# Weights kept as (high, low) pairs: the load of a weight tile takes every second element of 1024 bytes

## The chip, the cores and the metric

The kernel runs on one core of one Trainium2 chip. The metric is the device time of one execution in microseconds. The kernel before took 657.98 us (median of 3 runs, 657.59 to 659.76).

## The reference

Three layers follow each other; the matrices are float32 in the reference's arithmetic.

```python
# linear attention, q k v: (8, 8, 576, 64)
kv  = einsum('bhsd,bhse->bhde', softmax(k, over s), v)
x   = einsum('bhsd,bhde->bhse', softmax(q, over d), kv)   # -> 4608 tokens x 512
# feed-forward with a cosine gate, w_in: 512 x 2048, w_out: 2048 x 512
h = x @ w_in
x = (h * cos(h)) @ w_out
# soft mixture: 8 experts x 4 slots, w1: 512 x 1024, w2: 1024 x 512 each
logits = x @ phi
slot_input = softmax(logits, over tokens).T @ x
out = softmax(logits, over slots) @ experts(slot_input)
```

Only the product `h = x @ w_in` (4608 x 512 by 512 x 2048) touches the change.

## The kernel before, in words

The tokens are cut into nine blocks of 512. Stage by stage: block `b` of the attention gives a tile of x with 512 columns (tokens) and four chunks of 128 rows (`kk`); then sixteen steps follow, one for each 128 columns of `w_in` (`f`, 0 to 15). A step computes one 128 x 512 tile of `h` in PSUM (`mm1`, L925), rounds it, takes the fractional part, its cosine, and the product (L933 to L949); the results are the tile `G`, which feeds the logits (L963) and the weighted sums over tokens (L1110). The ninth block is worked in two halves of 256 tokens each, with tiles called `xe` instead of `XH` and `XL`. That is 8 x 16 steps with 512 columns and 2 x 16 with 256.

The product of a step is done in a three-term form. Both x and w are split into a high part (rounded to the type fp32r) and a low part (what the rounding left). For each chunk `kk` three matmuls add into the same PSUM tile: high w with high x, high w with low x, low w with high x. So a step is 4 x 3 = 12 matmuls, and each of them has a load of 128 x 128 weights of its own. In all there are 160 x 12 = 1920 loads and matmuls on L925: 1536 with 512 columns and 384 with 256.

The weights lie in eight tiles `W0` to `W7`, each of 256 columns of `w_in`, [128 partitions, 2 parts, 4 chunks, 256 columns]. A load of weights (`lhsT` on L925) reads 128 neighbouring elements of 4 bytes in each partition, that is 512 bytes.

How the W tiles come about: the weights arrive as 64-bit floats (two 32-bit words for each number). `conv_wi` turns 128 columns of them (one `f`) into 32-bit floats in a piece of the tile `A`; that takes a pass on ScalarE (L780), one on ScalarE or GpSimd that works on the neighbouring words of the raw data (L791, L795), and one on VectorE (L805). Then part 3 (L818, ScalarE) rounds `A` into the high part of W, and part 4 (L820, VectorE or GpSimd) subtracts that from `A` and writes the low part. There are sixteen of each, one for each `f`, between 19.7 and about 90 us; in this time the first block's steps run too.

What sets the order: every operation has a place in a list (`PLACES`), and the program is issued in the order of these places; which engine an operation takes is listed beside it (the string for `cD`, part 4, is "DDPPPDPDDPPPPPPP": D for VectorE, P for GpSimd). Waits between engines follow from the bytes that the operations read and write. For instance `cD` of f=7 has place 273, and the step of f=6 has 285; both touch the tile `W3`. A change of layout changes no place and no engine.

Of the kernel before, what the change touches and what calls it, by code (L numbers as in the profile page):

```python
# [10 lines left out]
F32 = mybir.dt.float32  # L11
F32R = mybir.dt.float32r
# [267 lines left out]
def attention_cosine_moe_softmoe(  # L280
# [21 lines left out]
    nc = tc.nc  # L302
# [10 lines left out]
    def sbt(shape, tag, dt=F32, bufs=1, name=None):  # L313
        if tag in PADS and tag not in PADDED:
            PADDED.add(tag)
            sb.tile([128, PADS[tag] // 4], F32, tag=f"pad{tag}", name=f"pad{tag}", bufs=1)
        return sb.tile(shape, dt, tag=tag, name=name or tag, bufs=bufs)

    def pst(tag, bufs):
        return ps.tile([128, 512], F32, tag=tag, name="ps_" + tag, bufs=bufs)  # L320
# [44 lines left out]
    w_t, xe = {}, []  # L365
# [402 lines left out]
    def convert(src, y, i, how):  # L768

        z = y.bitcast(I32)
        if not wide:
            if i == 0:
                nc.vector.tensor_copy(y, src[..., 0])
        elif i == 0:
            nc.scalar.activation(  # L780
                out=y, in_=src[..., 1].bitcast(F32), func=ACTF.Prelu, scale=2.0 ** -112,
                alpha=-(2.0 ** 32),
            )
        elif i == 1 and how == "DVE":
            nc.vector.tensor_scalar(
                out=z, in0=z, scalar1=3, scalar2=None, op0=ALU.logical_shift_left
            )
        elif i == 1:
            upper = src.bitcast(U16)[..., 1]
            if how == "ACT":  # L790
                nc.scalar.activation(  # L791
                    out=src[..., 0], in_=upper, func=ACTF.Identity, scale=2.0 ** -13, bias=low
                )
            else:
                nc.gpsimd.tensor_scalar(  # L795
                    out=src[..., 0], in0=upper, scalar1=2.0 ** -13, scalar2=LOW, op0=ALU.mult,
                    op1=ALU.add,
                )
        elif how == "DVE":
            nc.vector.scalar_tensor_tensor(  # L800
                out=z, in0=src[..., 0], scalar=29, in1=z, op0=ALU.logical_shift_right,
                op1=ALU.bitwise_or,
            )
        else:
            nc.vector.scalar_tensor_tensor(  # L805
                out=z, in0=z, scalar=3, in1=src[..., 0], op0=ALU.logical_shift_left,
                op1=ALU.bitwise_or,
            )

    def conv_wi(f, part, how):  # L810
        j, o = divmod(f, 2)
        o = slice(128 * o, 128 * o + 128)
        src = raw["i", j].rearrange("p k (f t) -> p k f t", t=RW)[:, :, o]
        t = abuf[:, 2 + f % 2].rearrange("p (k f) -> p k f", k=4)
        if part == 3:
            if j not in w_t:
                w_t[j] = sbt([128, 2, 4, 256], f"W{j}", F32R)
            nc.scalar.copy(out=w_t[j][:, 0, :, o], in_=t)  # L818
        elif part == 4:
            (nc.gpsimd if how == "POOL" else nc.vector).tensor_tensor(  # L820
                out=w_t[j][:, 1, :, o], in0=t, in1=w_t[j][:, 0, :, o].bitcast(F32),
                op=ALU.subtract,
            )
        else:
            convert(src, t, part, how)
# [63 lines left out]
    u_t, t_t, lt_t = {}, {}, {}  # L889
# [4 lines left out]
    def tile_of(d, i):  # L894

        return (i + (12 if 0 < d < 8 and d % 2 == 0 else 8 if d == 8 else 0)) % NF
# [14 lines left out]
    def mm1(s, ks):  # L911
        d, f = divmod(s, NF)
        b, t0, nt = parts[d]
        f = tile_of(d, f)
        if ks[0] == 0:
            u_t[s] = pst("h", 3)[:, 0:nt]
        w = w_t[f // 2]
        o = 128 * (f % 2)
        x = (
            (xh[b % 2], xl[b % 2]) if nt == 512  # L920
            else [xe[t0 // 256][:, i] for i in range(2)]
        )
        for kk in ks:
            for n, (wi, xi) in enumerate(((0, 0), (0, 1), (1, 0))):
                nc.tensor.matmul(  # L925
                    out=u_t[s], lhsT=w[:, wi, kk, o:o + 128], rhs=x[xi][:, kk],
                    start=(kk == 0 and n == 0), stop=(kk == 3 and n == 2),
                )

# [648 lines left out]
    def conv_ops():  # L1578
# [4 lines left out]
        for j, (ti, to) in enumerate(tags):  # L1583
            for kind, tag, load in (("i", ti, load_wi), ("o", to, load_wo)):
                mine = [(("cB" if kind == "i" else "oB"), f) for f in (2 * j, 2 * j + 1)]
                op(("lw" + kind, j), DMA, 2.75 if kind == "i" else 2.58, load, j, tag, more=LATE,
                   after=hold(tag, *mine))
            for f in (2 * j, 2 * j + 1):
                narrow("c", f, conv_wi, [("lwi", j), past("cD", f - 2)])
                op(("cH", f), ACT, 0.52, conv_wi, f, 3, ACT,  # L1590
                   after=[("cB", f)] + (hold(f"W{j}") if f % 2 == 0 else [("cH", f - 1)]))
                op(("cD", f), None, 0, conv_wi, f, 4, after=[("cH", f)],
                   ways=[(POOL, 1.26, True, ()), (DVE, 0.61, True, ())])
                narrow("o", f, conv_wo, [("lwo", j), past("w2_tr", f - 4), past("oW", f - 4)])
                op(("oW", f), DMA, 0.66, conv_wo, f, 3, None, more=LATE,
                   after=[("oB", f)])
                op(("w2_tr", f), PE, 0.47, w2_tr, f, take="m", after=[("oB", f)])
                op(("w2_tr_ev", f), None, 0, w2_tr_ev, f, give="m",
                   ways=[(ACT, 0.48, False, ()), (DVE, 0.6, False, ())],
                   after=[("w2_tr", f), past("w2_mm", j - 1)])  # L1600
            op(("w2_mm", j), PE, 0.52, w2_mm, j, take="m",
               after=[("w2_tr_ev", 2 * j), ("w2_tr_ev", 2 * j + 1), ("phi",), past("w2_ev", j - 1)])
            op(("w2_mm_ev", j), None, 0, w2_mm_ev, j,
               ways=[(ACT, 0.27, False, ()), (DVE, 0.33, False, ())],
               after=[("w2_mm", j), past("w2_sum", j - 2)])
            op(("w2_sum", j), PE, 0.35, w2_sum, j, duty=0.3, after=[("w2_mm_ev", j)])
            op(("w2_ev", j), DVE, 0.13, w2_ev, j, give="m", after=[("w2_sum", j)])
# [4 lines left out]
    def step_ops(s):  # L1612
# [13 lines left out]
        for ks in ((0,), (1,), (2,), (3,)) if s == 0 else (range(4),):  # L1626
            op(("mm1", s) if ks[-1] == 3 else ("mm1", s, ks[-1]), PE,
               (0.7 if nt == 512 else 0.355) * len(ks),
               mm1, s, ks, take=None if ks[0] else "h",
               after=[("x_lo", b, kk) for kk in ks] * (f == 0) + [past("cD", w)] * (b == 0)  # L1630
               + [("mm1", s, ks[0] - 1) if ks[0] else past("mm1", s - 1)]
               + [past("g", s - 3)] * (ks[0] == 0))
# [246 lines left out]
```

## Time and profile before

| | before |
|---|---|
| time, median of 3 runs | 657.98 us |
| the profiled execution's own time | 659.31 us |
| its span, first to last instruction | 657.4 us |
| mean granted TensorE clock in it | 0.986 |
| TensorE matmul (PE) busy | 625.2 us, 95% |
| TensorE weight loads (PEld) busy | 472.3 us, 72% |
| VectorE (DVE) busy | 534.9 us, 81% |
| ScalarE (ACT) busy | 365.6 us, 56% |
| GpSimd (POOL) busy | 128.2 us, 20% |

Busy times of PE and PEld overlap: a load of weights is recorded while the matmul before it runs. An instruction's recorded duration holds its latency, so that neighbours overlap; the pace of a stream is read from the starts of its instructions. The profiled execution's own time is 1.9 us above its span, and 1.33 us above the median of the runs.

### The profile page before, as it was taken

What the parts mean: (1) busy time and instruction counts of PE and PEld (TensorE: products, weight loads), DVE (VectorE), ACT (ScalarE), POOL (GpSimd) and SP (SyncE); (2) the same over time, 40 slices, a digit from 0 to 9 for tenths busy, and PEclk for the clock granted to TensorE, in tenths of its full rate; (3) what the DMA queues carried; (4) which work ended last, traced back from release to release, by engine and by line L of the source; (5) the groups of instructions that cost most, each with busy time, mean ns of one, the idle gap of its engine ahead of it and who ended that gap; (6) DMA issues with size and microseconds to landing.
All of it is one profiled execution on the core that took longest, in us unless ns stands there. A gap on an engine that the chain in (4) does not pass through costs nothing.

```text
span 657.4 us, 18204 instructions
## 1 busy us (share of the span) xinstructions
PE 625.2 (95%) x7745; PEld 472.3 (72%) x7745; DVE 534.9 (81%) x1075; ACT 365.6 (56%) x642; POOL 128.2 (20%) x131
## 2 busy tenths in 40 slices
PE   5999999999999999999999999999999999999990
PEld 4677777687868777877788788778878889853540
DVE  7889999989998988979979887878988888852251
ACT  4899988576465376446456452443645465530051
POOL 4435546052132043040230101001110000000000
PEclk9799999999999999999999999999999999999996
DMA  9998955264312242143212400013001518899968
GB/s 320 304 408 291 351 163 148 98 154 128 91 49 76 80 114 82 49 113 99 67 31 67 138 0 2 1 37 94 1 1 48 211 35 332 328 386 412 421 242 347
DMA packets 60992, 103.88 MB, mean 158 GB/s; under 512 B 9456, under 2 KB 40560, under 8 KB 55920
## 3 DMA queue, kind: packets, MB, share of 16 engines
q1 hardware_dynamic: 60912, 102.74, 45.9%
q8 instruction: 60, 0.98, 0.6%
q14 instruction: 20, 0.16, 0.1%
HBM read 88.15 MB, written 14.57 MB: 156 GB/s over the span
## 4 chain that ended last, share of the span: by engine, by line
PE 80%; DMA 7%; DVE 6%; ACT 2%; issue 1%; POOL 1%; SPq 0%; DVEq 0%; ACTq 0%
PE ps_h L925 54%; PE ps_m L1110 6%; PE ps_LT L963 4%; PE ps_m L713 2%; PE ps_m L528 2%; PE ps_m L1357 2%; DMA rwo<-in_moe_w_out_dram 2%; DMA Q<-in_q_dram 2%; PE ps_LT L1699 2%; DMA KVB<-in_k_dram 1%; DMA out_dram<-ob 1%; DMA G<-in_moe_w_out_dram 1%; PE ps_h L1315 1%; PE ps_m L1315 1%; DVE qm L422 1%
## 5 line engine op out<-in xcount | busy, mean ns | idle before, releaser
L925 PE MATMUL ps_h<-XH,W 128*128 128x512 f32 x1024 | 330.1, 397 | 2.2 <-DVE G L949 2.2
L925 PEld LDWEIGHTS ps_h<-XH,W 128*128 128x128 f32 x1024 | 192.3, 188 | 56.8 <-issue 7.1
L925 PE MATMUL ps_h<-XL,W 128*128 128x512 f32 x512 | 201.0, 393 | 0.0
L946 ACT ACTIVATE T<-T 128x512 f32<-128x512 f32 (+1 forms) x160 | 92.7, 587 | 90.8 <-DVE T L941 90.4
L933 ACT ACTIVATE T<-ps_h,quarter 128x512 int32<-128x512 f32 (+1 forms) x123 | 79.3, 646 | 87.0 <-PE ps_h L925 86.6
L949 DVE TENSOR_TENSOR G<-T,ps_h 128x512 f32<-128x512 f32 (+1 forms) x160 | 99.2, 623 | 21.0 <-ACT T L946 15.7
L925 PEld LDWEIGHTS ps_h<-XL,W 128*128 128x128 f32 x512 | 96.2, 188 | 20.0
L941 DVE SCALAR_TENSOR_TENSOR T<-T,ps_h 128x512 f32<-128x512 int32 (+1 forms) x160 | 98.9, 622 | 10.6 <-ACT T L933 9.4
L970 DVE STREAM_TRANSPOSE G<-G 128x512 f32<-128x512 f32 (+1 forms) x160 | 98.2, 637 | 0.3 <-PE ps_LT L963 0.2
L425 POOL TENSOR_TENSOR Q<-Q,qm 128x512 f32<-128x512 f32 x33 | 34.8, 1072 | 153.7 <-DVE qm L422 128.2
L689 POOL TENSOR_TENSOR KVB<-KVB,km 128x576 f32<-128x576 f32 x22 | 33.3, 1539 | 72.3 <-DVE km L682 51.3
L925 PE MATMUL ps_h<-xe,W 128*128 128x256 f32 x384 | 46.7, 281 | 0.0
L925 PEld LDWEIGHTS ps_h<-xe,W 128*128 128x128 f32 x384 | 45.3, 189 | 1.6 <-DVE G L949 0.8
L446 POOL TENSOR_TENSOR Q<-Q,qm 128x512 f32<-128x512 f32 x27 | 27.9, 1061 | 82.6 <-DVE qm L439 63.3
L963 PE MATMUL ps_LT<-G,wphi 128*32 128x128 f32 (+1 forms) x1280 | 38.7, 264 | 0.8 <-issue 0.8
L963 PEld LDWEIGHTS ps_LT<-G,wphi 128*32 128x32 f32 x1280 | 30.4, 109 | 8.9 <-issue 6.7
L1110 PE MATMUL ps_m<-G,A 32*32 32x512 f32 x1024 | 35.7, 597 | 0.0
L946 ACT ACT_TABLE_LOAD x24 | 30.8, 1283 | 0.4
L935 DVE TENSOR_SCALAR T<-ps_h 128x512 int32<-128x512 f32 (+1 forms) x37 | 22.7, 614 | 7.1 <-PE ps_h L925 6.9
L422 DVE TENSOR_REDUCE qm<-Q 128x8 f32<-128x512 f32 x36 | 24.0, 672 | 3.2 <-DMA Q<-in_q_dram 3.2
L1110 PEld LDWEIGHTS ps_m<-G,A 32*32 32x32 f32 x1024 | 16.9, 103 | 13.4 <-issue 8.1
L1128 DVE SCALAR_TENSOR_TENSOR gacc<-gacc,ac,ps_m 128x512 f32<-128x512 f32 x32 | 23.2, 732 | 2.3 <-PE ps_m L1110 2.3
(214 smaller groups left out, 715.6 us busy)
## 6 DMA issues: line engine op xcount, KB each, us to landing
w_u<-in_moe_w_dram SPq DMA_DIRECT2D x22, 1024.0 KB, 8.1
KVB<-in_k_dram SPq DMA_DIRECT2D x16, 576.0 KB, 5.1
KVB<-in_v_dram SPq DMA_DIRECT2D x32, 256.0 KB, 4.4
out_dram<-ob SPq DMA_DIRECT2D x8, 1024.0 KB, 8.9
rwi<-in_moe_w_in_dram SPq DMA_DIRECT2D x7, 1024.0 KB, 9.9
G<-in_moe_w_dram SPq DMA_DIRECT2D x7, 1024.0 KB, 7.0
rwo<-in_moe_w_out_dram SPq DMA_DIRECT2D x5, 1024.0 KB, 10.5
wo<-G SPq DMA_DIRECT2D x16, 256.0 KB, 4.5
```

The lines of the kernel that those rows point to most:

```text
L422: nc.vector.reduce_max(out=qm[:, t], in_=qv(t), axis=AX.X)
L425: (nc.vector if eng == "DVE" else nc.gpsimd).tensor_tensor(out=qv(t), in0=qv(t), in1=qm[:, t].unsqueeze(2).to_broadcast([128, 8, 64]), op= ...
L446: (nc.vector if eng == "DVE" else nc.gpsimd).tensor_tensor(out=qv(t), in0=qv(t), in1=qs[:, t].unsqueeze(2).to_broadcast([128, 8, 64]), op= ...
L689: (nc.vector if eng == "DVE" else nc.gpsimd).tensor_tensor(out=k_t[:, t], in0=k_t[:, t], in1=km[:, t].unsqueeze(1).to_broadcast([128, KC, ...
L925: nc.tensor.matmul(out=u_t[s], lhsT=w[:, wi, kk, o:o + 128], rhs=x[xi][:, kk], start=(kk == 0 and n == 0), stop=(kk == 3 and n == 2),)
L933: nc.scalar.activation(out=t.bitcast(I32), in_=u_t[s], func=ACTF.Identity, bias=quarter)
L941: nc.vector.scalar_tensor_tensor(out=t, in0=t.bitcast(I32), scalar=0.25, in1=u_t[s], op0=ALU.subtract, op1=ALU.subtract)
L946: nc.scalar.activation(out=t_t[s], in_=t_t[s], func=ACTF.Sin, scale=-UNDER_TWO_PI)
L949: nc.vector.tensor_tensor(out=g_of(s), in0=t_t.pop(s), in1=u_t.pop(s), op=ALU.mult)
L963: nc.tensor.matmul(out=lt_t[d][32 * c:32 * c + 32, 0:w], lhsT=w2sb[:, f], rhs=g[:, w * c:w * c + w], start=(f0 == 0), stop=(f0 == NF - 1),)
L970: nc.vector.transpose(out=g_of(s), in_=g_of(s))
L1110: nc.tensor.matmul(out=st["gp"][i][32 * c:32 * c + 32].rearrange("p (f b) -> p f b", f=NF) if d < NB else st["gp"][i][32 * c:32 * c + 32]. ...
```

## The change

The two parts become the innermost dimension of the W tiles: for each weight its high and its low part lie side by side, 4 bytes each. The size of a tile, its place, the number of instructions, their order and their engines stay. A load of weights now reads 128 elements with a step of two elements (8 bytes) over 1024 bytes; part 3 writes with that step, and part 4 reads one of its two inputs and writes with it.

```diff
         if part == 3:
             if j not in w_t:
-                w_t[j] = sbt([128, 2, 4, 256], f"W{j}", F32R)
-            nc.scalar.copy(out=w_t[j][:, 0, :, o], in_=t)
+                w_t[j] = sbt([128, 4, 256, 2], f"W{j}", F32R)
+            nc.scalar.copy(out=w_t[j][:, :, o, 0], in_=t)
         elif part == 4:
             (nc.gpsimd if how == "POOL" else nc.vector).tensor_tensor(
-                out=w_t[j][:, 1, :, o], in0=t, in1=w_t[j][:, 0, :, o].bitcast(F32),
+                out=w_t[j][:, :, o, 1], in0=t, in1=w_t[j].bitcast(F32)[:, :, o, 0],
                 op=ALU.subtract,
             )
...
         for kk in ks:
             for n, (wi, xi) in enumerate(((0, 0), (0, 1), (1, 0))):
                 nc.tensor.matmul(
-                    out=u_t[s], lhsT=w[:, wi, kk, o:o + 128], rhs=x[xi][:, kk],
+                    out=u_t[s], lhsT=w[:, kk, o:o + 128, wi], rhs=x[xi][:, kk],
                     start=(kk == 0 and n == 0), stop=(kk == 3 and n == 2),
                 )
```

## Rows read from the trace of the kernel before

**Rows 1.** The page: busy time of each engine; chain that ended last, by line.

```profile
PE 625.2 (95%) x7745; PEld 472.3 (72%) x7745; DVE 534.9 (81%) x1075; ACT 365.6 (56%) x642; POOL 128.2 (20%) x131
...
PE ps_h L925 54%; PE ps_m L1110 6%; PE ps_LT L963 4%; PE ps_m L713 2%; PE ps_m L528 2%; PE ps_m L1357 2%; DMA rwo<-in_moe_w_out_dram 2%; DMA Q<-in_q_dram 2%; PE ps_LT L1699 2%; DMA KVB<-in_k_dram 1%; DMA out_dram<-ob 1%; DMA G<-in_moe_w_out_dram 1%; PE ps_h L1315 1%; PE ps_m L1315 1%; DVE qm L422 1%
```

**Rows 2.** Stages: stretch, its us, busy us of engines, clock, DMA share, GB/s.

```profile
31.20:60.00 28.80, 28.02 (x158) 21.03 (x155) 26.65 (x48) 27.23 (x50) 12.41 (x14) 1.00 0.96 359
60.00:90.00 30.00, 30.00 (x383) 22.98 (x382) 29.38 (x56) 29.94 (x54) 15.57 (x13) 1.00 0.92 305
...
516.50:576.00 59.50, 59.50 (x848) 53.63 (x850) 50.74 (x140) 33.06 (x77) 0.00 (x0) 1.00 0.63 232
```

**Rows 3.** Weight loads by columns: busy us, mean ns of one, idle before.

```profile
L925 PEld LDWEIGHTS ps_h<-XH,W 128*128 128x128 f32 x1024 | 192.3, 188 | 56.8 <-issue 7.1 <-DVE G L949 5.0 <-DVE A L618 0.8
...
L925 PEld LDWEIGHTS ps_h<-xe,W 128*128 128x128 f32 x384 | 45.3, 189 | 1.6 <-DVE G L949 0.8 <-DVE cm L1152 0.2 <-issue 0.2
L963 PEld LDWEIGHTS ps_LT<-G,wphi 128*32 128x32 f32 x1280 | 30.4, 109 | 8.9 <-issue 6.7 <-DMA wo<-G 0.4
```

**Rows 4.** PE's timeline, first block's step f=8: start, us, what, count.

```profile
64.64 0.63 PE L925 MATMUL ps_h<-XH,W 128*128 128x512 f32 x2
65.10 0.39 PE L925 MATMUL ps_h<-XL,W 128*128 128x512 f32 x1
65.34 0.63 PE L925 MATMUL ps_h<-XH,W 128*128 128x512 f32 x2
```

**Rows 5.** PE's timeline, second block.

```profile
150.12 0.62 PE L925 MATMUL ps_h<-XH,W 128*128 128x512 f32 x2
150.57 0.39 PE L925 MATMUL ps_h<-XL,W 128*128 128x512 f32 x1
150.80 0.62 PE L925 MATMUL ps_h<-XH,W 128*128 128x512 f32 x2
```

**Rows 6.** PE's timeline, ninth block, 256 columns.

```profile
539.66 12.99 PE L925 MATMUL ps_h<-xe,W 128*128 128x256 f32 x108
552.58 1.10 PE L963 MATMUL ps_LT<-G,wphi 128*32 128x64 f32 x64
```

**Rows 7.** PE's timeline, transposes: two narrow windows of eight in a row.

```profile
40.74 0.49 PE L849 MATMUL ps_m<-ident,G 128*128 128x128 f32 x3
...
40.96 0.49 PE L849 MATMUL ps_m<-ident,G 128*128 128x128 f32 x3
```

**Rows 8.** The conversion's instructions by line: busy us, mean ns, idle before.

```profile
L820 POOL TENSOR_TENSOR W<-A,W 128x512 fp32r<-128x512 f32 x11 | 14.6, 1331 | 21.1 <-ACT W L818 17.5 <-DMA Q<-in_q_dram 3.4
L805 DVE SCALAR_TENSOR_TENSOR A<-A,rwi 128x512 int32<-128x512 int32 x14 | 10.1, 728 | 0.0
...
L818 ACT CAST W<-A 128x512 fp32r<-128x512 f32 x16 | 9.8, 617 | 1.6 <-DVE A L805 1.5
...
L791 ACT ACTIVATE rwi<-rwi,low 128x512 int32<-128x512 uint16 x8 | 6.1, 762 | 0.0
...
L820 DVE TENSOR_TENSOR W<-A,W 128x512 fp32r<-128x512 f32 x5 | 3.4, 683 | 0.2 <-ACT W L818 0.2
```

**Rows 9.** GpSimd's timeline, 22 to 46 us, of L453 and L820.

```profile
22.14 2.15 POOL L453 TENSOR_TENSOR B<-Q,qm 128x512 f32<-128x512 f32 x1 [7.25 <-PE ps_m L466]
...
44.20 1.30 POOL L820 TENSOR_TENSOR W<-A,W 128x512 fp32r<-128x512 f32 x1
```

**Rows 10.** PE's timeline, steps f=3 and f=4, around the start of f=4.

```profile
45.13 0.63 PE L925 MATMUL ps_h<-XH,W 128*128 128x512 f32 x2
45.60 0.39 PE L925 MATMUL ps_h<-XL,W 128*128 128x512 f32 x1
45.83 0.63 PE L925 MATMUL ps_h<-XH,W 128*128 128x512 f32 x2
```

**Rows 11.** PE's timeline, step f=6 from 55.58, and VectorE's, the low part of f=7.

```profile
55.58 0.50 PE L925 MATMUL ps_h<-XH,W 128*128 128x512 f32 x1
55.91 0.40 PE L925 MATMUL ps_h<-XL,W 128*128 128x512 f32 x1
56.15 0.63 PE L925 MATMUL ps_h<-XH,W 128*128 128x512 f32 x2
...
56.57 0.68 DVE L820 TENSOR_TENSOR W<-A,W 128x512 fp32r<-128x512 f32 x1
```

## The prediction

> **What bounds the kernel now.** Read the page's busy line first: TensorE's matmuls are busy for 95% of the span, and the chain that ended last runs for 54% of the span over L925, the very matmuls whose weights are re-laid [rows 1]. The reader should see that the change sits in the loop that sets the time. Then the stages: in the ninth block (516.5 to 576.0) PE is busy 59.50 of 59.50 us while VectorE, the next, has 50.74; whatever a pair of load and matmul loses there goes to the end in full. From 60 to 90 us PE and ScalarE are both full (30.00 and 29.94 of 30.00), and this is where half of the conversion runs [rows 2]. Last, the pace of the pairs, read from starts of matmuls, since their durations overlap. With 512 columns three pairs take 65.34 - 64.64 = 0.70 us in one block, 233 ns a pair [rows 4], and 150.80 - 150.12 = 0.68 us in another, 227 ns [rows 5]. With 256 columns 108 pairs take 552.58 - 539.66 = 12.92 us, 120 ns a pair [rows 6].
>
> **The change part by part.**
>
> *Loads of weights.* 1920 loads change their step from 4 to 8 bytes; none is added. How much room has a load? A record of 128 columns lasts 188 ns, one of 32 columns 109 ns [rows 3]: 79 ns for 96 columns, 0.82 ns a column, so 105 ns for 128, and the rest is latency that overlaps. Eight transposes show the same from another side: each has a load of 128 columns and a matmul short enough not to count, and two starts lie 40.96 - 40.74 = 0.22 us apart, 110 ns a pair [rows 7]. So a load of 128 columns holds the load path for about 105 to 110 ns. With 512 columns a pair takes 227 to 233 ns, and half of it is free on the load path: a load may double and still be covered by the matmul beside it. With 256 columns the pair takes 120 ns, so the cover is 10 ns. The whole question is thus whether a load of step 8 lasts longer, and the 384 pairs of the ninth block are the place that feels it first.
>
> No load of the trace has a step over one element, so I bound it. Low end: the step costs nothing, or the ninth block even falls to half the pace of the better 512-column stream (113 ns a pair), -(120 - 113) x 384 = -2.7 us. High end: every element costs as if the load read the skipped ones too, 256 columns in place of 128, so 2 x 110 = 220 ns. Under 512 columns that is covered (227 to 233); under 256 the pair becomes 220 ns in place of 120: 100 x 384 = 38.4 us, about +38. I take zero. The nearest rows are of VectorE: L805 reads one of its two inputs with a step of 8 bytes (one word of each 64-bit number) and takes 728 ns in the mean, L820 reads and writes without a step and takes 683 [rows 8]: half the elements of one input lie skipped, and the price is 7% at most, not 100%. That is another engine's port, and so only a hint.
>
> [...]
>
> *Pace of the matmuls.* The two paces, 227 and 233 ns, appear with the same loads of W; what differs between [rows 4] and [rows 5] is the block, that is the tile of x which streams. The moving operand is not touched, so I leave the mix as it is. If it were disturbed: with a mean near 230 (half way), all at 227 would give -3 x 1536 = -4.6 us, all at 233 +4.6 us.
>
> *Part 3, ScalarE.* 16 casts of 617 ns write with a step of 8 bytes. The nearest row is L791, which reads 2-byte words and writes 4-byte words, both with a step of 8 bytes: 762 ns [rows 8]. So a cast costs between 0 and 145 ns more; a gain is excluded, as the same elements pass. 13 of the 16 fall behind 31 us, where ScalarE is nearly full: at most 13 x 0.145 = 1.9 us, which reaches PE only if the steps' rounding and cosine on the same engine come late. PE is not waiting there (28.02 of 28.80, then 30.00 of 30.00 us busy) [rows 2]. I take zero, as the step of L791 is only one of the ways in which it differs; both ends are kept.
>
> *Part 4.* Five on VectorE: between 0 and 45 ns each by L805 against L820 [rows 8], at most 0.2 us, and VectorE is not what PE waits for in this stretch. Eleven on GpSimd of 1331 ns, which waited 21.1 us before them [rows 8], so its busy time is covered; only a low part that is awaited counts. The tightest is f=4: it ends at 44.20 + 1.30 = 45.50 [rows 9], and the third matmul of that step, the first with the low part, starts at 45.83, its load at the start of the one before, 45.60 [rows 10]. The cover is 0.10 us. No GpSimd row reads and writes two inputs with this step; the nearest that writes with a broken pattern is L453, at up to 2.15 us [rows 9]. So between 0 and 0.85 us more, less the cover: 0 to 0.75 us once; I take zero, the row without a change of bytes.
>
> *Waits.* High and low now share their byte range, and so do the two halves of a tile. A scheduler that compared ranges, not bytes, would add waits: the step of f=6 (issued after the low part of f=7, into the same tile) would wait for it. But in the trace that step starts at 55.58 and its first matmul with a low part at 56.15, while VectorE writes the low part of f=7 only from 56.57 [rows 11]. The ranges of these two already interleave over the four chunks before the change, and there was no wait; so bytes are compared, and I add none. If it came: the write ends at 56.57 + 0.68 = 57.25, so the step's first low matmul would be 1.1 us late, once.
>
> *Sum.* 0 for loads, 0 for pace, 0 (to 1.9) for part 3, 0 (to 1.0) for part 4, 0 (to 1.1) for waits. From the profiled execution's 659.3 us that gives 659.3; that execution lies 1.3 us above the median, which is what is timed again: 658.0. From the small one-sided ends I add about 0.4: 658.4.
>
> **The rivals.**
>
> *A. The load doubles* (slower). Place: the ninth block. It decides from the point at which a load lasts over about 120 ns, where a 256-column pair stops covering it. Price +38 us: 696. For it: the cover there is 10 ns. Against it: VectorE's reads with the same step pay 7% at most, and the load path takes one element in 0.82 ns while the moving operand, read from the same memory, takes one in 233 / 512 = 0.46 ns; a load of step 8 sweeps bytes no faster than the moving operand does already. This is my main reason.
>
> *B. The load is a quarter longer* (slower), because a part of its time goes with the bytes that it sweeps and not with the elements: 110 x 1.25 = 138 ns, 18 ns over the present pair, x 384 = 6.9 us: 665. [...]
>
> *C. Loads take turns with the moving operand* and every pair pays, the 1536 large ones too. The two paces show that 6 ns hang on something in the memory or the order; once more 6 ns on 1920 pairs would be +11.5 us: 670. Against it: the mix of paces follows x and not W.
>
> *D. The pace settles the other way*: all large pairs at 227 ns, -4.6 us, 653.4. For it and against it: as in C.
>
> *E. Loads far longer than doubled*, each element paying a full access: at three times, 330 ns, the large pairs pay 100 x 1536 = 154 us and the small 210 x 384 = 81 us: about 890. VectorE's rows speak against it.
>
> **How the numbers follow.** Forecast (nothing or below 2 us): 0.64. A 0.13, B 0.07, C 0.05, D 0.07, E 0.02, and 0.02 for small sums of parts 3 and 4 and a wait that together pass 2 us. A measurement of this kernel tells about 0.3%, 2 us, from no change. So faster 0.07, same 0.64, slower 0.29. The range goes from just below D, 652.5, to just above C, 675; outside are A and E, 0.15. The forecast's own range is 656 to 661.
>
> **What would show it.** If right: PE's starts on L925 keep 0.68 to 0.70 us for three, the ninth block's 108 pairs keep about 12.9 us, and the records of loads on L925 stay near 188 ns. Under A those records grow by some 100 ns and the ninth block by 38 us, while blocks one to eight keep their pace; under B the ninth block grows by 7 us; under C all blocks grow alike; under D blocks that go at 233 ns go at 227. ScalarE's casts on L818 at over 700 ns or GpSimd's on L820 at over 2 us would show the ends of parts 3 and 4. The prediction is wrong if a load's time follows the bytes that it sweeps.

## The result and the profile after

The changed kernel takes 664.78 us (median of 7 runs, 663.37 to 668.1) against 659.76 us (7 runs, 657.59 to 663.08) for the kernel before on the same chip: ratio 1.0081, 95% interval 1.0053 to 1.0109, some 5 us slower. The profiled execution, the fastest of the seven, took 663.37 us with a span of 661.4, 4.0 us more than the span before; the remaining 1.0 us between the medians lies outside what the two traces show.

The loads of weights by line (busy us, mean ns of one, idle before); compare [rows 3].

```profile
L925 PEld LDWEIGHTS ps_h<-XH,W 128*128 128x128 f32 x1024 | 198.7, 194 | 52.5 <-issue 7.1 <-DVE G L949 5.1 <-DVE A L618 0.8
...
L925 PEld LDWEIGHTS ps_h<-xe,W 128*128 128x128 f32 x384 | 46.8, 194 | 1.6 <-DVE G L949 0.8 <-DVE cm L1152 0.2 <-issue 0.2
L963 PEld LDWEIGHTS ps_LT<-G,wphi 128*32 128x32 f32 x1280 | 30.4, 109 | 8.5 <-issue 6.0 <-DVE A L805 0.3 <-DVE KVB L689 0.2
```

The loads on L925 grew from 188 to 194 ns, all 1920 of them in the mean; those of L963, which the change does not touch, stay at 109. PE's timeline in the second block (start, us, what, count), which answers to [rows 5], shows the pace of the pairs there:

```profile
147.61 0.63 PE L925 MATMUL ps_h<-XH,W 128*128 128x512 f32 x2
...
148.31 0.63 PE L925 MATMUL ps_h<-XH,W 128*128 128x512 f32 x2
```

Three pairs take 148.31 - 147.61 = 0.70 us where they took 0.68. In the third block, a block of the kind that went at 233 ns [rows 4], they now take 0.69, 230 ns a pair:

```profile
171.72 0.62 PE L925 MATMUL ps_h<-XH,W 128*128 128x512 f32 x2
...
172.41 0.62 PE L925 MATMUL ps_h<-XH,W 128*128 128x512 f32 x2
```

And the ninth block, as [rows 6], with the second of its two streams of 108 pairs behind it; the same stream of the kernel before stands in the second fence:

```profile
541.36 13.23 PE L925 MATMUL ps_h<-xe,W 128*128 128x256 f32 x108
554.52 1.10 PE L963 MATMUL ps_LT<-G,wphi 128*32 128x64 f32 x64
...
565.29 13.24 PE L925 MATMUL ps_h<-xe,W 128*128 128x256 f32 x108
578.45 0.65 PE L963 MATMUL ps_LT<-G,wphi 128*32 128x64 f32 x32
```

```profile
563.04 12.69 PE L925 MATMUL ps_h<-xe,W 128*128 128x256 f32 x108
575.66 0.65 PE L963 MATMUL ps_LT<-G,wphi 128*32 128x64 f32 x32
```

Both streams take 13.16 us now; before, the first took 12.92 and the second 12.62. In the trace before, the streams of this block go at about 113 or 118 ns from start to start and can switch between the two on the way; after the change they go at 120 throughout. The casts of the conversion (compare [rows 8]):

```profile
L818 ACT CAST W<-A 128x512 fp32r<-128x512 f32 x16 | 10.7, 679 | 0.6 <-DVE A L805 0.6
```

ScalarE's casts cost 62 ns more each, 679 in place of 617; the traces of e2, e3, e4 and e5, without the step in the conversion, have 616 to 630. VectorE's part went from 683 to 686 ns, and GpSimd's from 1331 to 1384. Neither is shown to be a price of the step: without it, GpSimd's part took 1342 to 1415 ns in the same four traces.

**Where the 4.0 us of the span are.** From the first to the last matmul on L925 it was 544.2 us and is 548.2, so all of it lies between these two points. The next table has the distance of neighbouring starts inside unbroken streams of pairs, averaged from the traces ("odd": the second, fourth, sixth and eighth block, whose x lies in XH1 and XL1; "even": the first, third, ..., in XH0 and XL0).

| kernel | load, ns | odd blocks | even blocks | 256 columns | L925, first to last |
|---|---|---|---|---|---|
| before | 188 | 227.8 | 233.3 | 116.1 | 544.2 us |
| changed | 194 | 233.2 | 231.1 | 120.1 | 548.2 us |
| conversion stepped (e1) | 188 | 227.8 | 233.3 | 115.4 | 545.1 us |
| loads stepped (e2) | 194 | 233.2 | 230.7 | 120.1 | 547.5 us |
| neither, blocks (e3) | 188 | 227.8 | 233.3 | 115.1 | 542.8 us |
| loads stepped, one part (e5) | 194 | 233.2 | 230.7 | 120.1 | 546.9 us |
| conversion stepped, one part (e6) | 188 | 227.7 | 233.3 | 117.1 | 542.9 us |
| x moved by 64 bytes (e8) | 188 | 227.7 | 232.5 | 118.7 | 544.0 us |
| only low loads stepped (e10) | 190 | 231.1 | 233.1 | 120.0 | 546.0 us |
| only high loads stepped (e11) | 193 | 232.3 | 233.1 | 119.1 | 547.4 us |
| step 3 (e7) | 255 | 234.4 | 233.4 | 178.4 | 573.4 us |
| step 4 (e4) | 314 | 235.1 | 238.0 | 236.6 | 606.5 us |
| step 8 (e9) | 331 | 244.6 | 245.3 | 243.9 | 617.9 us |

By this table: odd blocks (233.2 - 227.8) x 768 = +4.1 us, even blocks (231.1 - 233.3) x 768 = -1.7, ninth block (120.1 - 116.1) x 384 = +1.5, and the first pair of each of the 39 streams with 512 columns, 341.6 in place of 332.5 ns, +0.4: together +4.3 for the 4.0 measured. The paces of the 512-column blocks come back to within 1 ns in every other trace with the same kind of load, but the sum does not close to better than about 2 us: the times between the streams differ from trace to trace (the kernel before and e3 have the same 512-column paces and lie 1.4 us apart). The 256-column pairs without a step differ too, 115.1 to 118.7 ns from trace to trace, so that the ninth block's share lies between 0.5 and 1.9 us.

### The profile page after: what moved, and what is told of

Read it like the earlier page. It is cut to its first block, busy times and chain, and to the rows that moved or that the text cites. A ratio compares the mean times of both kernels' runs of the same rounds, so it can differ in the third digit from the quotient of the medians.

```text
span 661.4 us, 18204 instructions
## 1 busy us (share of the span) xinstructions
PE 629.7 (95%) x7745; PEld 483.4 (73%) x7745; DVE 535.1 (81%) x1075; ACT 366.6 (55%) x642; POOL 128.6 (19%) x131
## 4 chain that ended last, share of the span: by engine, by line
PE 75%; DMA 8%; DVE 8%; ACT 4%; issue 2%; SPq 1%; POOL 1%; DVEq 0%; ACTq 0%; POOLq 0%
PE ps_h L925 53%; PE ps_m L1110 6%; PE ps_LT L963 4%; PE ps_m L713 3%; DMA w_u<-in_moe_w_dram 3%; PE ps_m L528 2%; DMA G<-in_moe_w_dram 1%; DMA out_dram<-ob 1%; DMA KVB<-in_k_dram 1%; DMA Q<-in_q_dram 1%; PE ps_LT L1699 1%; SPq L401 1%; DVE G L949 1%; PE ps_m L849 1%; DVE T L941 1%
## 5 line engine op out<-in xcount | busy, mean ns | idle before, releaser
L925 PE MATMUL ps_h<-XH,W 128*128 128x512 f32 x1024 | 331.6, 398 | 2.9 <-DVE G L949 2.9
L925 PEld LDWEIGHTS ps_h<-XH,W 128*128 128x128 f32 x1024 | 198.7, 194 | 52.5 <-issue 7.1
L925 PE MATMUL ps_h<-XL,W 128*128 128x512 f32 x512 | 201.6, 394 | 0.0
L925 PEld LDWEIGHTS ps_h<-XL,W 128*128 128x128 f32 x512 | 99.5, 194 | 17.8
L925 PE MATMUL ps_h<-xe,W 128*128 128x256 f32 x384 | 48.1, 284 | 0.0
L925 PEld LDWEIGHTS ps_h<-xe,W 128*128 128x128 f32 x384 | 46.8, 194 | 1.6 <-DVE G L949 0.8
L963 PE MATMUL ps_LT<-G,wphi 128*32 128x128 f32 (+1 forms) x1280 | 38.8, 264 | 0.3 <-issue 0.3
L963 PEld LDWEIGHTS ps_LT<-G,wphi 128*32 128x32 f32 x1280 | 30.4, 109 | 8.5 <-issue 6.0
```

The source lines that it names most:

```text
L925: nc.tensor.matmul(out=u_t[s], lhsT=w[:, kk, o:o + 128, wi], rhs=x[xi][:, kk], start=(kk == 0 and n == 0), stop=(kk == 3 and n == 2),)
L963: nc.tensor.matmul(out=lt_t[d][32 * c:32 * c + 32, 0:w], lhsT=w2sb[:, f], rhs=g[:, w * c:w * c + w], start=(f0 == 0), stop=(f0 == NF - 1),)
```

## The experiments

Theory 1: the stepped load is longer and moves the pace of the pairs. Theory 2: the slower conversion delays the first blocks. Theory 3: it is where the parts lie, not the step.

**The step in the conversion alone (e1).** To the changed kernel:

```diff
-                    out=u_t[s], lhsT=w[:, kk, o:o + 128, wi], rhs=x[xi][:, kk],
+                    out=u_t[s], lhsT=w[:, kk, o:o + 128].rearrange("p f t -> p (f t)")[
+                        :, 128 * wi:128 * wi + 128], rhs=x[xi][:, kk],
```

> The conversion writes high and low as pairs, with the step of 8 bytes, as in the changed kernel, but a load reads 128 neighbouring elements (the first or the second half of the same 1024 bytes, so the product is of mixed high and low parts). Theory 1 (the stepped load costs: its record grew from 188 to 194 ns and the pace of the pairs changed): loads back at 188 ns, odd blocks of L925 at 227 ns a pair and the 256-column pairs at 113 to 118 ns as before the change; ratio 1.000 to the kernel before. Theory 2 (the slower conversion costs, ScalarE's casts having grown from 617 to 682 ns): casts still at about 680 ns, ratio 1.006 to 1.008.

Measured: 662.72 us, ratio 1.0052 (1.0028 to 1.0077). Loads and paces are those of the kernel before, as theory 1 has it, but the time is not. The profiled execution was the fastest of 12 (660.46 us) and does not show the rest. One thing was in this run that is not in the changed kernel: its blocks mix both parts, so the first high load of a step depends on the low part too.

**The step in the loads alone (e2), and neither (e3).** To the kernel before; e3 is the same layout with the second form of the load:

```diff
-                w_t[j] = sbt([128, 2, 4, 256], f"W{j}", F32R)
-            nc.scalar.copy(out=w_t[j][:, 0, :, o], in_=t)
+                w_t[j] = sbt([128, 4, 2, 2, 128], f"W{j}", F32R)
+            nc.scalar.copy(out=w_t[j][:, :, f % 2, 0], in_=t)
...
+                    # e2: every second element of the block
+                    lhsT=w[:, kk, f % 2].rearrange("p w (c t) -> p (w c) t", t=2)[:, :, wi]
+                    # e3: neighbours
+                    lhsT=w[:, kk, f % 2, wi]
```

> The conversion writes 128 neighbouring elements at a time, high and low of one chunk in one block of 1024 bytes; a load reads every second element of that block, as in the changed kernel, byte for byte (so the product is of mixed high and low parts). Theory 1: loads at 194 ns, odd blocks at 233 ns, the 256-column pairs at 120 ns, ratio 1.006 to 1.008. Theory 2: ratio 1.000, with casts at 617 ns.

> The same blocks of 1024 bytes as in the kernel with the stepped load alone, but both conversion and loads go over neighbouring elements (the product is the reference's). Theory 1: as the kernel before, ratio 1.000, loads at 188 ns. Theory 3 (it is the place of the parts in memory, not the step, that sets the pace of the matmuls): the pace moves as in the changed kernel, odd blocks at 233 ns, ratio 1.005 or more, though loads last 188 ns.

Measured: e2 668.59 us, ratio 1.0114 (1.0073 to 1.0155); e3 659.13 us, ratio 0.9982 (0.9965 to 0.9999). Theory 3 falls: the same blocks without a step are not slower. Theory 1's paces come with the step in the load and with nothing else: 194 ns, 233.2, 120.1. But e1 is above e3, clear of noise, and e2's median is above the changed kernel's, though the intervals of these two overlap; e1 and e2 both have loads that mix the parts. In e2's waits of the load queue from 28 to 100 us (who waited for whom, us, times, longest) there is one for the low part that the changed kernel doesn't have:

```profile
PEld ps_h L925 <- POOL W L820: 0.6, 1, 0.6
```

**The same two halves without that wait (e5, e6).** Blocks of one part, two chunks each. e5 writes neighbours and loads with the step; e6 writes with the step and loads neighbours.

```diff
+                w_t[j] = sbt([128, 2, 2, 512], f"W{j}", F32R)
+            # e5
+            nc.scalar.copy(out=w_t[j][:, f % 2, 0].rearrange("p (k c) -> p k c", k=4), in_=t)
+                    lhsT=w[:, f % 2, wi, 256 * (kk // 2) + kk % 2:256 * (kk // 2) + 256:2]
+            # e6
+            nc.scalar.copy(out=w_t[j][:, f % 2, 0].rearrange("p (g c t) -> p g t c", g=2, t=2),
+                           in_=t.rearrange("p (g t) c -> p g t c", g=2))
+                    lhsT=w[:, f % 2, wi, 128 * kk:128 * kk + 128]
```

> As the run with the stepped load alone, but each load reads every second element of a block that holds one part only (two chunks of the high or of the low part, written by neighbouring elements; the product is of swapped chunks). So a high load doesn't wait for the low part, as it did in the two runs whose blocks hold both parts. If that wait made these two slow (about 0.4%), this run has the load's price alone: theory 1: loads at 194 ns, odd blocks 233 ns, 256-column pairs 120 ns, loop 4 us longer, ratio 1.006 to 1.008, below the 1.0114 of the earlier run. Theory 2 (the load costs nothing that lasts): 1.000 to 1.002.

> The other half: the conversion writes with a step of 8 bytes (two chunks of one part are interleaved), loads read 128 neighbouring elements (the product is of mixed chunks of one part), and a high load doesn't wait for the low part. Theory 1: the casts at about 680 ns are hidden, ratio 0.998 to 1.002, below the 1.0052 of the earlier run. Theory 2: 1.004 to 1.006, the conversion has a price of its own of 2 to 4 us.

Measured: e5 664.21 us, ratio 1.0071 (1.0044 to 1.0097), e6 658.99 us, ratio 0.9993 (0.9976 to 1.0011). The step in the load alone has the whole effect within the intervals; the step in the conversion alone has none, though e6's casts are as slow as the changed kernel's (675 ns; e5's take 628). Three pairs of the second block take 0.70 us in e5 (first fence) and 0.68 us in e6 (second); behind them stand e6's casts and loads, and e5's loads:

```profile
147.00 0.63 PE L926 MATMUL ps_h<-XH,W 128*128 128x512 f32 x2
...
147.70 0.63 PE L926 MATMUL ps_h<-XH,W 128*128 128x512 f32 x2
```

```profile
149.97 0.62 PE L926 MATMUL ps_h<-XH,W 128*128 128x512 f32 x2
...
150.65 0.62 PE L926 MATMUL ps_h<-XH,W 128*128 128x512 f32 x2
```

```profile
L818 ACT CAST W<-A 128x512 fp32r<-128x512 f32 x16 | 10.7, 675 | 0.4 <-DVE A L805 0.4
...
L926 PEld LDWEIGHTS ps_h<-xe,W 128*128 128x128 f32 x384 | 45.6, 189 | 1.6 <-DVE G L950 0.8 <-DVE cm L1153 0.2 <-issue 0.2
```

```profile
L926 PEld LDWEIGHTS ps_h<-xe,W 128*128 128x128 f32 x384 | 46.8, 194 | 1.6 <-DVE G L950 0.8 <-DVE cm L1153 0.2 <-issue 0.2
```

So theory 2 falls. If the 3.4 us of e1 belonged to the conversion, the changed kernel, which converts in the same way, should lie at e5's price and this together, near 1.012; it is at 1.0081. What e1 and e2 have on top may be the wait for the low part, but this is not shown: the wait in e2's trace is 0.6 us long, e1's trace has none on L820, and both traces are of the fastest executions of their kernels, which lie 2 to 6 us below the medians.

**How the load depends on the step (e4, e7, e9).** Steps of 4, 3 and 8 elements. The form for step 4, in blocks of two chunks with both parts (e9: one block of four chunks, `t=8`; e7: `lhsT=w[:, f % 2, wi, kk:kk + 382:3]` in e5's layout):

```diff
+                w_t[j] = sbt([128, 2, 4, 2, 128], f"W{j}", F32R)
+                    lhsT=w[:, f % 2, 2 * (kk // 2):2 * (kk // 2) + 2].rearrange(
+                        "p k w (c t) -> p (k w c) t", t=4)[:, :, 2 * (kk % 2) + wi]
```

The pieces of 16 bytes in the theories of these three runs are a supposition of the author's; no run before them shows such a size.

> The conversion writes neighbouring elements into blocks of 2048 bytes (two chunks, high and low), and a load reads every fourth element of such a block, a step of 16 bytes (the product is of mixed parts). Theory 1a (the load's extra time goes with the bytes swept, 6 ns for 512 more): 1024 more than at step 2, so loads at about 205 ns; the pair of 256 columns at 125 to 132 ns, +4 us on top of the changed kernel, ratio about 1.013 to 1.017. Theory 1b (a fixed price for any step): loads at 194 ns, ratio 1.006 to 1.008. Theory 1c (two elements on 16 bytes are the limit for a load at full speed): at one element on 16 bytes a load lasts twice as long, the 256-column pair about 220 ns, +38 us, ratio 1.06.

> Loads of every third element, a step of 12 bytes, over 1532 bytes of one part (the product is of mixed chunks). Step 1: 188 ns, step 2: 194, step 4: 314 measured. Theory L (the load path takes a new piece of 16 bytes in about 1.7 ns, and 128 elements in 105 ns, and the longer of both counts): 96 pieces take 160 ns in place of 107 at step 2, so the load is at about 245 to 255 ns and the 256-column pair at 170 to 180 ns. Theory M (any step over two elements is one fetch for each element): the same as at step 4, 314 and 236 ns.

> Loads of every eighth element, a step of 32 bytes, over 4096 bytes of both parts (the product is of mixed parts). So far: step 1: 188 ns, 2: 194, 3: 255, 4: 314; the 256-column pair at 116, 120, 178, 237 ns. Theory P (a load pays for each piece of 16 bytes that it touches, some 1.87 ns; 64, 96 and 128 pieces fit 120, 178 and 237): 128 elements touch 128 pieces at any step from 4, so step 8 is as step 4, 314 and 237 ns. Theory S (a load pays for the bytes swept, 60 ns for each 512 from step 2 on): 314 + 4 x 60 = 554 ns, the pair at about 475 ns, and the 512-column blocks at about 475 ns too.

Measured: step 4 720.15 us, ratio 1.0897 (1.0857 to 1.0937); one execution each of step 3, 689.26 us, and of step 8, 733.35 us. The ninth block's stream of 108 pairs in the three traces, in the order 3, 4, 8:

```profile
552.44 19.34 PE L926 MATMUL ps_h<-xe,W 128*128 128x256 f32 x108
571.71 1.10 PE L964 MATMUL ps_LT<-G,wphi 128*32 128x64 f32 x64
```

```profile
570.88 25.48 PE L925 MATMUL ps_h<-xe,W 128*128 128x256 f32 x108
596.29 1.10 PE L963 MATMUL ps_LT<-G,wphi 128*32 128x64 f32 x64
```

```profile
579.95 26.38 PE L925 MATMUL ps_h<-xe,W 128*128 128x256 f32 x108
606.26 1.10 PE L963 MATMUL ps_LT<-G,wphi 128*32 128x64 f32 x64
```

13.16 us at step 2 become 19.27, 25.41 and 26.31. From step 2 to 4 each further element costs a load 60 ns (194, 255, 314), and there it ends: twice the bytes, at step 8, cost 17 ns more (331), not 240. At step 4 theory 1c comes nearest (a pair of 236.6 ns for its 220, a ratio of 1.0897 for its 1.06), and 1a and 1b fall. At step 3 theory M falls: there is no cliff behind two elements but an even rise, as theory L had it (255 ns and 178.4 for its 245 to 255 and 170 to 180). At step 8 theory S (bytes swept) falls, and theory P, a price for each piece of memory touched, is left, though it had no rise at all from step 4 to 8, and there were 17 ns a load and 7.3 ns a pair. The size of a piece was not measured by itself. What the runs give is where the rise ends: at (236.6 - 120.1) / 2 = 58 ns an element a 256-column pair comes to step 8's 243.9 ns at 4.1 elements, some 16.5 bytes, an estimate, as no step between 4 and 8 was run. If a piece is 16 bytes, 128 elements touch 32, 64, 96, 128 and 128 pieces at steps 1, 2, 3, 4 and 8, and the 256-column pairs at 120.1, 178.4, 236.6 and 243.9 ns at steps 2, 3, 4 and 8 are 1.88, 1.86, 1.85 and 1.91 ns a piece. By this fit a load at step 2 would hold the load path for 120 ns against the 110 ns of a load without a step [rows 7], just more than the 115 to 119 ns of a 256-column pair without a step. At steps 3 and 4 the pair's 178.4 and 236.6 ns stand well above those 115 to 119; for step 2 the price is an estimate from the fit, and the next two runs do not bear it out load by load.

Two elements on 16 bytes, theory 1c's limit for a load at full speed, are not quite free: step 2 adds 6 ns to a record of 188 and 4.0 ns to a 256-column pair of 116.1. Steps 3 and 4 add 67 and 126 ns to the record.

**Only a third, or two thirds, of the loads stepped (e10, e11).** In e5, the step only where `wi` is 1 (low), or only where it is 0 (high).

> Only the loads of low parts, one of three, have the step of 8 bytes; blocks of one part (the product has swapped chunks in its low term). Theory P, each load paying for itself: a third of the 256-column pairs at 120 ns and the others as before (113 to 118), mean 115 to 119; in the 512-column blocks the odd ones between 227 and 233 ns, about 229. Rival (a stream of pairs has one pace, which any stepped load shifts): odd blocks at 233 ns and the 256-column pairs at 120 ns as if all loads were stepped.

> Only the loads of high parts, two of three, have the step of 8 bytes; blocks of one part (the product has swapped chunks in its high terms). Theory P: mean of the 256-column pairs 117 to 120 ns, odd blocks about 231. Rival: 233 and 120 ns.

Measured, one execution each: 660.95 and 661.70 us, beside 658.53 for the kernel before. The ninth block is slow at 120.0 and 119.1 ns with a third or two thirds of the loads stepped, as the rival has it; odd blocks lie between (231.1, 232.3), as theory P has it; even blocks stay at 233.1 and don't fall to 231. So neither holds whole. The pairs of a stream are slow together: in e10's ninth block the starts of a chunk's three matmuls and of the next chunk's first lie 121, 121 and 118 ns apart, though only one of the three loads is stepped. The fall in the even blocks to 231 ns showed only with all loads at step 2 (231.1 in the changed kernel, 230.7 in e2 and e5).

**The place of x (e8).** In the kernel before:

```diff
-    PADS = {'wphi': 32}
+    PADS = {'XH0': 64, 'wphi': 96}
```

> The kernel before with its layout of weights, and XH0 and XL0, the tiles of x of the even blocks, moved by 64 bytes so that they begin on a multiple of 128 as XH1, XL1 and the W tiles do (everything behind them moves by 128). If the place of x within 128 bytes sets the pace of the pairs: even blocks at 227 ns in place of 233, 768 x 6.6 ns = 5 us, ratio 0.992. If it doesn't: even blocks stay at 233 ns, ratio 1.000.

Measured: 660.54 us, ratio 1.0026 (1.0004 to 1.0048). Even blocks go at 232.5 ns, not 227: the place of x within 128 bytes isn't what divides the blocks. What does was not isolated: odd and even blocks differ in their tiles of x, but also in the part of `G` that they write and in the work beside them.

## Why the prediction was right or wrong

The time, 664.8 us, lies in the range, but not where the forecast stood (658.4, no change, 0.64), nor in its own range of 656 to 661. Slower had 0.29. The range held the result because of the prices of rivals B and C, not because of the sum; that B's 665 is the number measured is luck, since B put all of it into the ninth block, which has 1.5 us of it.

- *The place and the bound* were right: the 4.0 us of the span lie between the first and the last matmul of L925.
- *Loads, "I take zero"*: this term failed. The reason for it, that the load path could sweep the bytes as the moving operand does, compared the wrong things: the records grew from 188 to 194 ns, and at steps 3 and 4 to 255 and 314. The ninth block, where the cover was thinnest, lost 4.0 ns a pair, +1.5 us. The cover of 10 ns was read from one of the two long streams, 120 ns; the other, which [rows 6] doesn't have, went at 12.62 / 108 = 117 ns. This is rival B's place and sign at a fifth of its price (+6.9), but not its reason: "follows the bytes that it sweeps" falls at step 8 (331 ns where theory S had 554). Its quarter of a load was an estimate that no run shows; the records grew by 6 ns of 188. Rival A's +38 us lies near what step 4 costs in that block, (236.6 - 116.1) x 384 = +46 us.
- *Pace, "I leave the mix as it is"*: this step failed too, and it is the larger half. I argued that the two paces follow x and not W. They change with the load of W too: with the step, odd blocks go from 227.8 to 233.2 (+4.1 us) and even ones from 233.3 to 231.1 (-1.7 us). Rival C had pace and load hang together, but with one price for every pair (+11.5 us), and half of the large pairs became faster; the net of the large pairs is +2.4. A load of 120 ns, the fit's estimate, has room in a pair of 230, and still the odd blocks lost 5.4 ns a pair; so cover alone did not say that it costs nothing.
- *Part 3*: 62 ns a cast, inside 0 to 145, and hidden, as costed (e6). *Part 4*: 53 ns on GpSimd in the mean, which lies within its scatter from trace to trace, 3 ns on VectorE; hidden. *Waits*: none on the conversion was added.
- The hint from VectorE's rows said nothing about TensorE's loads, and was not firm: L805's 728 ns, against which the 7% were read, are 693 in the trace after.

**What stays open.** Why pairs of 512 columns have these paces at all. It is not the place of x within 128 bytes (e8), nor the place of the parts (e3). The steps of the ladder are small (227, 230, 233 ns), and most of a stream keeps to one; which one goes with the parity of the block and with the loads' step together. The runs show that the loads' step moves it, not by what.

## What to carry to other kernels

In this kernel a load of weights that steps over elements wasn't free even at step 2 (194 ns for 188, 120.1 ns for 116.1 in a 256-column pair, ratio 1.0081): price it against the shortest matmul that has to cover it, and test it there. The streams of matmuls and loads had two paces in the trace before, 227.8 and 233.3 ns, and the step in the loads moved the odd blocks to 233.2 and the even ones to 231.1; a few nanoseconds on 1900 pairs are several microseconds, so where a trace has two paces, the range should hold both. Keep hi/lo parts, or chunks, apart by whole loads: blocks side by side cost nothing here (e3, ratio 0.9982).

## What was not expected of the hardware

- A load of 128 columns: 188, 194, 255, 314 and 331 ns in the mean at steps of 1, 2, 3, 4 and 8 elements of 4 bytes (before, changed, e7, e4, e9).
- ScalarE's cast of 128 x 512 took 617 ns to neighbours (before) and 679 ns with a step of 8 bytes at the output (changed); VectorE's subtraction took 683 ns without and 686 ns with such an output and one such input.
- Pairs of load and 512-column matmul held one of a few paces (227, 230 or 233 ns) through most of a stream, and a step of 8 bytes in the loads changed which one: 227.8 to 233.2 ns in odd blocks, 233.3 to 231.1 in even ones.
